# VectorE takes its branch over the general program six operations before its last one, and SyncE issues the last store

## The chip, the core and the metric

The kernel runs on one NeuronCore of a Trainium2 chip. The core has five engines with an instruction stream each: TensorE (PE in the profile, its weight loads PEld), VectorE (DVE), ScalarE (ACT), GpSimd (POOL) and SyncE (SP), which does nothing but issue DMAs and wait. The metric is the device time of one launch in microseconds; lower is better.

## The reference

The input is 2048 rows of 448 features in bf16. The kernel computes `h2 = h + B(LN(h))` with `h = x + A(LN(x))`, where

- A is sliding-window attention: 16 heads of 28, each row looks at 8 rows of its past, two apart, and the result goes through a 448 x 448 matrix;
- B is an MLP mixer: layer norm, a 448 x 448 matrix and gelu, a shift of each quarter of the features by -1, +1, -2 or +2 rows, a second 448 x 448 matrix, a residual; then layer norm, 448 x 1792, gelu, 1792 x 448, and a residual.

```python
h  = x + A(layernorm(x), A_wqkv, A_wo)
z  = layernorm(h)
x1 = z + shift(gelu(layernorm(z) @ w1)) @ w2
h2 = h + x1 + gelu(layernorm(x1) @ w3) @ w4
```

The change touches the order of instructions, and none of the arithmetic.

## The kernel before, in words

The program holds two versions of the computation. The **fast program** (`_fast_path`, L452) takes a short cut in the chain of layer norms that holds for ordinary numbers. It also computes a **flag** (`phase_flag`, L969): whether any variance was infinite or not a number. The **general program** (`_general_path`, L1072) makes no such assumption. Every engine runs its part of the fast program to the end, reads the flag from SBUF into a register (L1514), and jumps over its part of the general program when the flag is zero (L1515). With these inputs the flag is zero. So each engine makes one taken branch, across as many instructions as its part of the general program has. For SyncE these are the DMAs of the general program: 17 in each of four attention stages (L1318 to L1323), 16 stores, and the loads. VectorE, ScalarE and above all TensorE have more.

After the branch comes `finish` (L1484): an engine that issued output stores waits until they have landed. Then all five engines meet in a barrier at the end of the block (L1508): each drains and counts up a semaphore, GpSimd waits for all of them and releases them.

The fast program is written as operations with dependencies. A list scheduler (`_Sched.schedule`, L234) puts them in an order by its own cost estimates and by ranks written out by hand (L1042 to L1068). `_emit_plan` (L416) then finds the semaphore waits, and `emit` (L1468) writes each engine's instructions; all of them carry the line L1476 in the profile.

The end of the fast program is the second MLP matrix, `phase_W4` (L949). For each group of 128 rows, TensorE runs 14 matmuls (one for each 128 of the 1792 hidden features) into one PSUM bank of 128 x 448; VectorE adds the residual and writes bf16 to `xb` (L961); a DMA stores the rows. For the last 512 rows (`u == 3`) each group has a store of its own (L963). The very last group is cut in two halves of 224 columns. SyncE stores the first half, ScalarE's queue the second:

```python
dma("out%d_%d_%d" % (m, a, n0), bass.AP(out.tensor, ...), xb[:, i, n0:n1],
    128 * n * 2, q="sp" if n0 == 0 else "act")
```

TensorE's last nine groups feed VectorE's last nine operations, which are all residual adds. I call them add 1 to add 9; adds 8 and 9 are the two halves. The planner gives the groups two PSUM banks in turn, so that TensorE's group 6 waits until VectorE has done add 4, and so on. ScalarE's last activation ends about 20 us before the end, and GpSimd has finished about 57 us before it.

Of the kernel before, what the change touches and what calls it, by code (L numbers as in the profile page):

```python
# [415 lines left out]
def _emit_plan(S, order, sems, chan_sems):  # L416
    cnt = {}
    for e, lst in order.items():
        c = 0
        for op in lst:  # L420
            if op.is_dma:
                k = cnt.get(op.chan, 0) + 1
                cnt[op.chan] = k
                op.sem = chan_sems[op.chan]; op.val = 16 * k
            elif op.users > 0:
                c += 1
                op.sem = sems[e]; op.val = c
    eclock = {e: {} for e in order}
    plan = {}
    for op in S.gorder:  # L430
        cur = eclock[op.eng]
        waits = []
        for d in sorted(op.deps, key=lambda d: -d.t1):
            key = id(d.sem)
            if cur.get(key, 0) >= d.val:
                continue
            waits.append((d.sem, d.val))
            new = dict(cur)
            for k2, v2 in d.clock.items():
                if new.get(k2, 0) < v2:  # L440
                    new[k2] = v2
            cur = new
        eclock[op.eng] = cur
        plan[op.idx] = waits
        oc = dict(cur)
        if op.sem is not None:
            oc[id(op.sem)] = max(oc.get(id(op.sem), 0), op.val)
        op.clock = oc
    return plan


def _fast_path(nc, es, flag, A_x, A_wqkv, A_wo, B_w1, B_w2, B_w3, B_w4, out):  # L452
# [9 lines left out]
    S = _Sched()  # L462
# [51 lines left out]
    def dve(meth, dur, **kw):  # L514
        return S.add("dve", meth, dur, **kw)
# [17 lines left out]
    def dma(chan, out_ap, in_ap, nbytes, dur=450.0, rate=200.0, q="sp", after=(), bulk=False, lat=1200.0):  # L533
        if chan[0] == "w":
            chan = ch(chan)
        op = S.macro(q, [("dma_start", dict(out=out_ap, in_=in_ap))], dur, chan=chan, lat=(lat, nbytes / rate, 1150.0),
                     after=tuple(after) + tuple(last) if chan[0] in "xw" else after, bulk=bulk)
        if chan[0] in "xw":
            last[:] = [op]
        if chan[0] == "o":  # L540
            op.deps -= {d for d in op.deps if d.is_dma}
        return op

    def tile(n=1):
        g = _Group(n)
        return lambda fn: _PV(g, lambda b: fn(ps[:, b:b + n, :]))

    def mm(out_ap, lhsT, rhs, start, stop, **kw):
        return ("matmul", dict(out=out_ap, lhsT=lhsT, rhs=rhs, start=start, stop=stop, **kw))

    def pe(ins, dur, mode, after=()):
        return S.macro("pe", ins, dur, mode=mode, after=after)
# [3 lines left out]
    def xrows(ap, m):  # L556
        return bass.AP(ap.tensor, 256 * m * D, [[2 * D, 128], [1, 2 * D]])
# [391 lines left out]
    def phase_W4(u):  # L949
        for k in range(2):  # L950
            m = 2 * u + k
            for a in range(2):
                S.tag = "W4_%d_%d" % (u, k)
                i = 2 * m + a
                for n0, n1 in ((0, 224), (224, D)) if (u, k, a) == (3, 1, 1) else ((0, D),):
                    n = n1 - n0
                    T = tile()
                    ins = [mm(T(lambda p, n=n: p[:, 0, 0:n]), h3T[u % 2][:, f, a, 128 * k:128 * k + 128], w4_s[:, f, n0:n1], f == 0,
                              f == NF - 1) for f in range(NF)]
                    w4s.append(pe(ins, 14 * (n / 2.4 + 2.5), "full", after=w4s if n < D else ()))  # L960
                    dve("tensor_tensor", (150 + n) / 0.96, out=xb[:, i, n0:n1], in0=T(lambda p, n=n: p[:, 0, 0:n]),  # L961
                        in1=xb[:, i, n0:n1], op=ALU.add)
                    if u == 3:  # L963
                        dma("out%d_%d_%d" % (m, a, n0), bass.AP(out.tensor, 256 * m * D + a * D + n0, [[2 * D, 128], [1, n]]), xb[:, i, n0:n1],
                            128 * n * 2, q="sp" if n0 == 0 else "act")
            if u < 3:
                dma("out%d" % m, xrows(out, m), xb[:, 2 * m:2 * m + 2, :].rearrange("p a n -> p (a n)"), 128 * D * 4)

    def phase_flag():  # L969
        S.tag = "flag"  # L970
        bits = mv[:, 1, :, :].rearrange("p i s -> p (i s)").bitcast(I32)
        dve("tensor_scalar", 150, out=fint[:], in0=bits, scalar1=23, scalar2=255, op0=ALU.logical_shift_right,
            op1=ALU.bitwise_and)
        dve("tensor_reduce", 180, out=fmax[:], in_=fint[:], axis=AX.X, op=ALU.max)
        dve("tensor_scalar", 120, out=fbit[:], in0=fmax[:], scalar1=254.5, scalar2=None, op0=ALU.is_ge)
        T = tile()
        w4s.append(pe([mm(T(lambda p: p[0:1, 0, 0:1]), fbit[:], ones[:, 0:1], True, True)], 60, "c32"))
        return dve("tensor_scalar", 200, out=flag[0:1, 0:1], in0=T(lambda p: p[0:1, 0, 0:1]), scalar1=16.0,
                   scalar2=None, op0=ALU.mult)
# [45 lines left out]
    phase_W3(0)  # L1025
    wo_ln2(3, 4)
    phase_W4(0)
    wo_ln2(5, 6)
    phase_W1(3, 4)
# [3 lines left out]
    w2_ln3(4, 5)  # L1033
    phase_W1(7, 1)
    phase_W4(1)
    flag_op = phase_flag()
    w2_ln3(6, 7)
    phase_W3(2)
    phase_W4(2)
    phase_W3(3)  # L1040
    phase_W4(3)
# [419 lines left out]
def _plan(nc, es, S, prefix):  # L1461
    order = S.schedule()
    S.settle()
    sems = {e: es.enter_context(nc.semaphore(prefix + "sem_" + e)) for e in order}
    chan_sems = {c: es.enter_context(nc.semaphore(prefix + "d_" + c)) for c in S.chan_count}
    plan = _emit_plan(S, order, sems, chan_sems)

    def emit(e, eng):  # L1468
        out_final = {}
        for op in order.get(e, []):  # L1470
            if op.load is not None:
                eng.preload_act_table_set(_TABLE_SETS[op.load])
            for (sem, val) in plan[op.idx]:
                eng.wait_ge(sem, val)
            for meth, kw in op.ins:
                inst = getattr(eng, meth)(**kw)  # L1476
            if op.is_dma:
                inst.then_inc(op.sem, 16)
                if op.chan.startswith("out"):
                    out_final[op.chan] = max(out_final.get(op.chan, 0), op.val)  # L1480
            elif op.users > 0:
                inst.then_inc(op.sem, 1)

        def finish():  # L1484
            for c, v in out_final.items():
                eng.wait_ge(chan_sems[c], v)
        return finish
    return emit
# [5 lines left out]
def bass_sequential_preLN__sliding_local_dilated__mixer_s_mlp__prompt_kernel(  # L1494
    nc, A_x, A_wqkv, A_wo, B_x, B_w1, B_w2, B_w3, B_w4, out,
):
    args = (A_x, A_wqkv, A_wo, B_w1, B_w2, B_w3, B_w4, out)
    with ExitStack() as es:
        flag = es.enter_context(nc.sbuf_tensor("flag", [1, 1], I32))
        gate = es.enter_context(nc.semaphore("gate"))  # L1500
        with ExitStack() as es1:
            S, flag_op = _fast_path(nc, es1, flag, *args)
            flag_op.users += 1
            emit_fast = _plan(nc, es, S, "f_")
            _LAST["S"] = S
        with ExitStack() as es2:
            emit_general = _plan(nc, es, _general_path(nc, es2, *args), "g_")
            with nc.Block() as block:  # L1508
                for e in _ENG:
                    def body(eng, e=e):  # L1510
                        finish = emit_fast(e, eng)
                        eng.wait_ge(flag_op.sem, flag_op.val)
                        with eng.register("redo_" + e) as reg:
                            eng.reg_load(reg, flag[0:1, 0:1])  # L1514
                            with eng.If_ne(reg, 0):  # L1515
                                finish()
                                eng.drain().then_inc(gate, 1)
                                eng.wait_ge(gate, len(_ENG))
                                emit_general(e, eng)()
                        finish()  # L1520
                    getattr(block, _ENG[e])(body)

# [27 lines left out]
```

## Time and profile before

| | |
|---|---|
| runs | 199.91, 201.06, 201.94, 202.78 us; median 201.5 us |
| profiled execution, its own time | 201.94 us |
| profiled execution, span from the first to the last instruction | 200.2 us |
| around the span | 1.7 us |
| TensorE matmul busy | 186.1 us (93%) |
| VectorE busy | 119.8 us (60%) |
| ScalarE busy | 105.8 us (53%) |
| GpSimd busy | 49.9 us (25%) |
| instruction packets, queue q8 | 27, 0.44 MB |
| instruction packets, queue q14 | 8, 0.07 MB |

Busy time counts work on data alone. Register loads, branches, waits and the issuing of DMAs are an engine's sequencer's work; the profile lists them by source line with an engine name that ends in q (DVEq, ACTq). The difference of two starts on such lines tells how long the engine stood between them. Queues q1 and q10 carry SyncE's and ScalarE's data, q8 and q14 carry instructions that are fetched for the engines.

### The profile page before, as it was taken

Reading aid. Unit: us, or ns where it says so; the run is one execution under the profiler, and the core shown is the slowest. Engines: PE = TensorE matmul, PEld = TensorE weight load, DVE = VectorE, ACT = ScalarE, POOL = GpSimd, SP = SyncE. Lnnn points to the kernel's source line nnn. Section 1 sums busy time; section 2 is a strip of 40 time slices with the busy share of each in tenths; the row PEclk is TensorE's granted clock in tenths of the full one; section 3 lists DMA queues with packets and bytes.
Section 4 is the critical chain, followed back from the end, with each engine's and each line's share of the span. In section 5 each row is a group of like instructions: output and inputs, shape, how many; then the busy total and the mean of one; then the engine's idle time right before and its main releaser. Section 6 shows DMA issues by size and latency. Waiting matters only on the chain.

```text
span 200.2 us, 6997 instructions
## 1 busy us (share of the span) xinstructions
PE 186.1 (93%) x3150; PEld 117.6 (59%) x3151; DVE 119.8 (60%) x294; ACT 105.8 (53%) x120; POOL 49.9 (25%) x89
## 2 busy tenths in 40 slices
PE   7789999999997998979998999999999999999990
PEld 2458666455453464538854465588887558755570
DVE  6899797677999249999998039998000210021130
ACT  3586799975699688485631731156466006600000
POOL 6211430000082000594633002979500000000000
PEclk9999999999999699999999999999999999999999
DMA  6967575444368423355452300424400011001111
GB/s 182 362 238 104 114 157 100 141 120 127 99 129 131 128 66 114 108 101 135 137 96 46 95 0 0 93 49 101 89 0 3 0 46 49 3 0 46 69 46 37
DMA packets 31851, 18.32 MB, mean 92 GB/s; under 512 B 21640, under 2 KB 31240, under 8 KB 31816
## 3 DMA queue, kind: packets, MB, share of 16 engines
q1 hardware_dynamic: 31128, 17.30, 35.1%
q8 instruction: 27, 0.44, 1.0%
q10 hardware_dynamic: 688, 0.52, 0.9%
q14 instruction: 8, 0.07, 0.1%
HBM read 9.75 MB, written 1.84 MB: 58 GB/s over the span
## 4 chain that ended last, share of the span: by engine, by line
PE 53%; DVE 27%; DMA 8%; POOL 6%; issue 1%; ACT 1%; DVEq 0%
PE ps L1476 53%; DVE st L1476 8%; DMA HT<-ln 7%; DVE xb L1476 5%; DVE ln L1476 4%; POOL rstd L1476 4%; DVE xin L1476 2%; POOL xb L1476 2%; DVE QK L1476 2%; DVE mv L1476 2%; DVE nmr L1476 1%; DVE arena L1476 1%; DMA xin<-in_A_x_dram 1%; DVE pt L1476 1%; DVE w_s L1476 1%
## 5 line engine op out<-in xcount | busy, mean ns | idle before, releaser
L1476 PE MATMUL ps<-HT,w_s 64*128 64x256 bf16 (+3 forms) x952 | 57.7, 280 | 2.6 <-DMA HT<-ln 2.3
L1476 PEld LDWEIGHTS ps<-HT,w_s 64*128 64x128 bf16 x952 | 45.3, 95 | 14.7 <-DMA HT<-ln 3.3
L1476 DVE TENSOR_TENSOR xb<-ps,xb 128x448 bf16<-128x448 f32 (+2 forms) x25 | 18.6, 747 | 57.2 <-PE ps L1476 57.2
L1476 PE MATMUL ps<-HT,arena 64*128 64x128 bf16 (+2 forms) x448 | 27.2, 270 | 0.6 <-DMA HT<-ln 0.4
L1476 POOL TENSOR_SCALAR vtmp<-mv 128x2 f32<-128x2 f32 x30 | 6.1, 203 | 84.5 <-DVE mv L1476 78.8
L1476 ACT ACTIVATE arena<-ps 128x1024 bf16<-128x1024 f32 x14 | 14.3, 1024 | 16.9 <-PE ps L1476 16.9
L1476 PE MATMUL ps<-w_s,h 128*128 128x448 bf16 x112 | 21.9, 353 | 0.0
L1476 PE MATMUL ps<-w_s,arena 128*128 128x448 bf16 (+1 forms) x126 | 21.7, 332 | 0.0
L1476 POOL TENSOR_TENSOR rstd<-vtmp,mhalf 128x2 f32<-128x2 f32 x30 | 21.0, 701 | 2.3
L1476 ACT ACTIVATE QK<-ps 128x1024 bf16<-128x1024 f32 (+2 forms) x19 | 18.6, 979 | 5.6 <-PE ps L1476 5.3
L1476 PEld LDWEIGHTS ps<-HT,arena 64*128 64x128 bf16 x448 | 16.6, 94 | 8.3 <-DMA HT<-ln 0.9
L1476 ACT ACTIVATE h<-ps 128x1024 bf16<-128x1024 f32 x14 | 14.3, 1023 | 8.2 <-PE ps L1476 8.2
L1476 DVE BATCH_NORM_STATS2 st<-xin 128x6 f32<-128x448 bf16 x32 | 18.4, 609 | 0.4 <-DMA xin<-in_A_x_dram 0.4
L1476 PEld LDWEIGHTS ps<-w_s,arena 128*128 128x128 bf16 x126 | 12.2, 98 | 9.2 <-issue 0.2
L1476 PEld LDWEIGHTS ps<-w_s,h 128*128 128x128 bf16 x112 | 10.9, 98 | 10.3 <-issue 0.2
L1476 POOL TENSOR_TENSOR xb<-xb,xin 128x448 bf16<-128x448 bf16 x16 | 16.1, 1034 | 1.0 <-DVE ln L1476 1.0
L1476 ACT ACTIVATE pt<-ps 128x912 bf16<-128x912 f32 x18 | 15.7, 927 | 1.2 <-PE ps L1476 1.1
L1476 PE MATMUL ps<-wo_s,QK 128*128 128x448 bf16 x64 | 13.0, 353 | 1.7 <-DVE xin L1476 1.3
L1476 DVE TENSOR_TENSOR QK<-ps,lnz 128x456 bf16<-128x456 f32 (+1 forms) x24 | 10.8, 507 | 6.3 <-PE ps L1476 6.2
L1476 PE MATMUL ps<-wv_s,HT 64*128 64x448 bf16 x126 | 13.1, 350 | 0.6 <-DVE wv_s L1476 0.6
L1476 PE MATMUL ps<-w_s,QK 112*128 112x448 bf16 x64 | 12.6, 353 | 0.0
L1476 DVE TENSOR_SCALAR ln<-xin,mv,rstd 128x448 bf16<-128x448 bf16 x25 | 11.8, 496 | 0.6 <-ACT rstd L1476 0.6
(67 smaller groups left out, 190.6 us busy)
## 6 DMA issues: line engine op xcount, KB each, us to landing
w_s<-in_B_w_dram SPq DMA_DIRECT2D x19, 224.0 KB, 2.6
xin<-in_A_x_dram SPq DMA_DIRECT2D x7, 224.0 KB, 6.5
out_dram<-xb SPq DMA_DIRECT2D x6, 224.0 KB, 2.8
vu<-vt SPq DMA_DIRECT2D x9, 128.0 KB, 2.7
h<-in_A_wqkv_dram SPq DMA_DIRECT2D x3, 336.0 KB, 5.2
wv_s<-in_A_wqkv_dram SPq DMA_DIRECT2D x2, 336.0 KB, 6.6
w_s<-in_B_w_dram SPq DMA_DIRECT2D x2, 336.0 KB, 3.2
wo_s<-in_A_wo_dram SPq DMA_DIRECT2D x4, 98.0 KB
```

What stands on the lines that cost most here:

```text
L1476: inst = getattr(eng, meth)(**kw)
```

## The change

The store of the second half goes to SyncE's queue like all other stores. For VectorE alone, the fast program is cut in front of its last six operations. The register load and the branch come at the cut. The six operations stand twice in the program: at the head of the general branch, and behind it under the opposite condition. The other engines branch at their end as before.

```diff
                     if u == 3:
                         dma("out%d_%d_%d" % (m, a, n0), bass.AP(out.tensor, ...), xb[:, i, n0:n1],
-                            128 * n * 2, q="sp" if n0 == 0 else "act")
+                            128 * n * 2)
...
-    def emit(e, eng):
+    def emit(e, eng, lo=0, hi=None):
         out_final = {}
-        for op in order.get(e, []):
+        for op in order.get(e, [])[lo:hi]:
...
             emit_fast = _plan(nc, es, S, "f_")
+            dve = [op for op in S.gorder if op.eng == "dve"]
+            late = max(len(dve) - 6, dve.index(flag_op) + 1)
...
                     def body(eng, e=e):
-                        finish = emit_fast(e, eng)
+                        cut = late if e == "dve" else None
+                        finish = emit_fast(e, eng, 0, cut)
                         eng.wait_ge(flag_op.sem, flag_op.val)
                         with eng.register("redo_" + e) as reg:
                             eng.reg_load(reg, flag[0:1, 0:1])
                             with eng.If_ne(reg, 0):
+                                if cut is not None:
+                                    emit_fast(e, eng, cut)
                                 finish()
                                 eng.drain().then_inc(gate, 1)
                                 eng.wait_ge(gate, len(_ENG))
                                 emit_general(e, eng)()
+                            if cut is not None:
+                                with eng.If_eq(reg, 0):
+                                    emit_fast(e, eng, cut)
                         finish()
```

## The prediction

> **What bounds the kernel now.** I first read the chain of waits for the last 60 us. It is one piece of TensorE work that ends in VectorE's last add:
>
> ```profile
> 5 pieces in order of time: start us, us, what
> ...
> 141.82 53.72 PE ps L1476 x574
> 195.54 0.02 issue
> 195.56 0.39 DVE xb L1476
> ```
>
> From 141.8 to 195.5 TensorE runs without a hole, and the work on data ends at 195.95. The span ends at 200.2. So there are two places to look at: the 4.3 us behind the last add, where this change acts, and the rhythm of the last adds, into which it puts a branch. The timeline of the last stretch shows the rhythm:
>
> ```profile
> 182.29 0.62 DVE L1476 TENSOR_TENSOR xb<-ps,xb 128x448 bf16<-128x448 f32 x1 [2.02 <-PE ps L1476]
> ...
> 184.94 0.62 DVE L1476 TENSOR_TENSOR xb<-ps,xb 128x448 bf16<-128x448 f32 x1 [2.02 <-PE ps L1476]
> 187.58 0.63 DVE L1476 TENSOR_TENSOR xb<-ps,xb 128x448 bf16<-128x448 f32 x1 [2.02 <-PE ps L1476]
> ...
> 195.56 0.39 DVE L1476 TENSOR_TENSOR xb<-ps,xb 128x224 bf16<-128x224 f32 x1 [0.95 <-PE ps L1476]
> 195.99 0.36 ACTq L1476 DMA_DIRECT2D out_dram<-xb  x1
> ```
>
> These are adds 3, 4, 5 and 9 and the last store. VectorE works 0.62 us and waits 2.02 us for TensorE. Third, the instructions of the register load, the branch and the final barrier, by line:
>
> ```profile
> L1514 SPq TENSOR_LOAD <-flag x1: 525/525/525, 195.0 to 195.0; - x1
> L1514 DVEq TENSOR_LOAD <-flag x1: 546/546/546, 195.6 to 195.6; - x1
> L1514 ACTq TENSOR_LOAD <-flag x1: 474/474/474, 196.4 to 196.4; - x1
> ```
>
> ```profile
> L1515 PEldq COMPARE_BRANCH  x1: 4818/4818/4818, 194.3 to 194.3; - x1
> L1515 SPq COMPARE_BRANCH  x1: 63/63/63, 195.6 to 195.6; - x1
> L1515 DVEq COMPARE_BRANCH  x1: 72/72/72, 196.2 to 196.2; - x1
> L1515 ACTq COMPARE_BRANCH  x1: 59/59/59, 196.9 to 196.9; - x1
> ```
>
> ```profile
> L1508 SPq DRAIN  x1: 13/13/13, 199.0 to 199.0; - x1
> L1508 DVEq DRAIN  x1: 58/58/58, 199.1 to 199.1; - x1
> L1508 PEldq DRAIN  x1: 73/73/73, 199.2 to 199.2; - x1
> L1508 ACTq COMPARE_BRANCH  x1: 38/38/38, 199.8 to 199.8; - x1
> L1508 ACTq DRAIN  x1: 8/8/8, 200.0 to 200.0; - x1
> ```
>
> A branch counts as tens of ns, but the time to the engine's next instruction is the price: VectorE 196.16 to 199.08 and ScalarE 196.89 to 199.82, 2.92 us each; TensorE 4.82. SyncE branches at 195.60 and has its next instruction at 195.80, GpSimd's is 0.17 us behind its branch: 0.2 us or less. In the packet records a fetch of 8 KB on the instruction queue q14 starts 1.04 us behind VectorE's branch and 1.18 behind ScalarE's and takes 0.47 and 0.40 us, and the engine goes on 1.4 us after that. TensorE's has 16 KB on q8 and takes 2.03 us. So three engines jump to code that must be fetched, and two to code that is there.
>
> The engines reach the barrier in the order SyncE 199.00, VectorE 199.08, TensorE 199.21, ScalarE 199.98. **ScalarE is last.** Its chain is: add 9 ends 195.95, store issued 195.99 to 196.35, register load 196.39 to 196.86, branch 196.89, fetch to 199.82, drain 199.98, end of the span 200.22.
>
> **The change part by part.**
>
> *The store leaves ScalarE.* ScalarE's last activation ends at 175.26. Its load (0.47) and branch (2.92) then end before 179, 17 us before add 9, which covers them. Its entry at 199.98 vanishes. If the cover were gone it would pay the 3.4 us again.
>
> *The store joins SyncE.* SyncE's store of the first half was issued by 194.97, so its queue is free. It now waits for add 9, at 195.99, and issues in 0.33 us (its own row for the first half), to 196.32. Behind that wait stand its register load, its branch and its waits for the stores. Load 0.525: 196.88. Branch: 196.95, and 0.2 by its own row: 197.15. Then it waits for the landing. Before, 14 of the 16 parts of the last store had landed at 197.54 and the two last at 198.68 and 198.92, because those two DMA engines also carried TensorE's fetches. In SyncE's queue the store stands behind the first half, which landed at 198.76; before it was carried out behind that one too, from another queue. I leave the landing at 198.92; the bounds are 0.4 earlier (VectorE's fetch of 0.47 us is no longer beside it) and 0.3 later (56 KB, whose packets span about that time on the late engine). SyncE's drain began 0.24 behind its last landing, which gives 199.17.
>
> *VectorE's branch moves to the cut.* The cut is behind add 3. The register load was issued 0.01 us after add 9 had started, so now at 182.30; it ends at 182.85. Branch 182.88. The target is fetched: 2.92, to 185.81. The second branch is not taken: 0.2 by SyncE's row. Add 4 starts at 186.0 instead of 184.94 and ends at 186.6. Six adds are queued behind the branch. Who waits: SyncE's store of add 4 (1.1 us late; its next is due at 188.24, nothing collides), and TensorE, whose group 6 starts at 187.19 and needs the bank of add 4. That leaves 0.5 us of cover. Add 5 is due at 187.58 anyway. Cost: nothing. For the fetch the bounds are 2.9 us (VectorE's own row) and 4.8 (TensorE's); a gain here is excluded, since no add can start before its matmuls. I take 2.9: same engine, same jump.
>
> [...] If VectorE's fetch were like q8's, 4.8 us, it would go on at 187.7, add 4 would end at 188.5, and group 6 would start 1.4 us late. [...]
>
> *What VectorE gains at its end.* Its entry moves from 199.08 to about 196.1. TensorE enters at 199.21 either way, so this half of the change is worth nothing by itself.
>
> **Sum.** The last entry becomes TensorE's: its branch needs add 7 (end 193.50) and neither edit moves it. Its drain ends at 199.28, ScalarE's ended at 199.99: 0.71 us less. The profiled execution had 201.94 for a span of 200.2; with the same 1.7 us around it I get 201.94 - 0.71 = 201.23. It lies 0.44 above the median of the runs, so **on the scale of the median 201.5 becomes 200.8 us**.
>
> **The rivals.**
>
> *A, slower: the stall reaches TensorE.* [...] The place is the bank of add 4; it decides once VectorE resumes later than about 186.5, which is 3.7 us after its branch. Two fetches in series are 5.84: 188.7, add 4 ends at 189.55, and TensorE, with no hole until its end, is 2.4 us late. 200.8 + 2.4 = 203.2 us. For it: TensorE's row of 4.8 is beyond that point. Against it: VectorE's and ScalarE's rows agree at 2.92 with one packet each.
>
> *B, no change: SyncE inherits the fetch.* One DMA and one wait more stand in its stream; if its target falls out of what is loaded, it continues at 196.95 + 2.92 = 199.87, just where ScalarE did: 201.5 us. Against it: the jump grows by an instruction or two among some hundred.
>
> *C, more is gained.* With two fetches out of the last 4 us, the late store parts and TensorE's fetch of 2.03 us (undisturbed q8 packets took 0.9) may shorten, and part of the 1.7 us around the span may hold fetches of the closing code, whose packets stand at 199.7 to 201.2. The first is worth up to 0.5, the second at most about as much: 199.9 us. No view shows either.
>
> That the change doesn't do what it says is no real case: which engine branches where follows from the program.
>
> **How the numbers follow.** My forecast has a chance of 0.62, A 0.14, B 0.11, C 0.13. The four runs spread from 199.91 to 202.78, so a median carries about 0.7 us of its own. The range is 199.6 to 202.7: it takes in the forecast, B, most of C, and A at its lower bound of 1.4 us (202.2). One per cent, 2.0 us, is about what a measurement of this kernel can tell from no change. Faster than that needs C with luck: 0.07. Slower needs A at its full price or beyond: 0.11. Within it: 0.82.
>
> **What would show it.** Right: ScalarE's and VectorE's rows of the branch stand near 176 and 182.9; VectorE resumes 2.9 us later; add 4 starts near 186.0 and add 5 at its old place; TensorE's piece has no hole; the drains stand in the order ScalarE, VectorE, SyncE, TensorE, the last at 199.2, and the span is 199.5. Wrong: idle time of TensorE before group 6 (A); SyncE's first wait on L1486 only near 199.9 (B); TensorE's drain well before 199.0 (C). A hole anywhere before 182 would mean that something else moved.

## The result, and the profile after

The changed kernel takes 197.83 us (median of 12 runs, 196.49 to 202.29), the kernel before beside it 201.06 us (17 runs). The ratio is 0.989, 95% interval 0.985 to 0.993. Compared a second time, the ratio was 0.9935 (0.9907 to 0.9962). So the change saves 1.3 to 2.2 us, where I had forecast 0.7. On the scale of the 201.5 us shown above, the first comparison gives 199.3 us, below my range. The ratios count only executions within 1.5% of the fastest of their kernel; the profiled ones of before and of `pe_plus12` (below) are slower than that, so of these two only the end and the time outside the span are used.

The chain of waits for the last stretch, of the kernel after (start, length, what):

```profile
...
139.94 53.33 PE ps L1476 x570
...
193.29 0.39 DVE xb L1476
```

TensorE has no hole from 139.9 to 193.3, so VectorE's branch in the middle of the adds cost TensorE nothing. The timeline shows where the branch stands, with adds 3, 4, 5 and 9:

```profile
180.01 0.62 DVE L1476 TENSOR_TENSOR xb<-ps,xb 128x448 bf16<-128x448 f32 x1 [2.02 <-PE ps L1476]
...
183.52 0.62 DVE L1476 TENSOR_TENSOR xb<-ps,xb 128x448 bf16<-128x448 f32 x1 [2.88 <-PE ps L1476]
185.31 0.63 DVE L1476 TENSOR_TENSOR xb<-ps,xb 128x448 bf16<-128x448 f32 x1 [1.16 <-PE ps L1476]
...
193.29 0.39 DVE L1476 TENSOR_TENSOR xb<-ps,xb 128x224 bf16<-128x224 f32 x1 [0.95 <-PE ps L1476]
```

Add 4 starts 3.51 us behind add 3 instead of 2.65, so it is 0.86 late. Add 5 stands 5.30 behind add 3, which is twice 2.65: on time. Now the branches (L1518 here) and the entries into the last barrier (L1510):

```profile
L1518 ACTq COMPARE_BRANCH  x1: 50/50/50, 172.5 to 172.5; - x1
L1518 DVEq COMPARE_BRANCH  x1: 72/72/72, 180.6 to 180.6; - x1
L1518 PEldq COMPARE_BRANCH  x1: 3420/3420/3420, 191.9 to 191.9; - x1
L1518 SPq COMPARE_BRANCH  x1: 62/62/62, 195.0 to 195.0; - x1
```

```profile
L1510 ACTq DRAIN  x1: 81/81/81, 175.1 to 175.1; - x1
L1510 DVEq DRAIN  x1: 430/430/430, 193.3 to 193.3; - x1
L1510 PEldq DRAIN  x1: 72/72/72, 195.4 to 195.4; - x1
...
L1510 SPq DRAIN  x1: 13/13/13, 195.8 to 195.8; - x1
```

The order is the one I had named, except that SyncE comes last and TensorE, which I had put at the end, arrives 0.4 before it. And both are much closer to the end of the work. I count from the start of add 9 on, because the two profiles differ by 2.27 us before it, in stretches that the change doesn't touch. (The profiled execution of before had one stretch of 3.4 us at a granted TensorE clock of 0.5, that of after had none; but this isn't shown to be the reason, for `act_early`, further down, had such a stretch too and reached add 9 at 192.41.) From add 9 to the end of the span it is 4.66 us before (195.56 to 200.22) and 2.89 after (193.29 to 196.18). I call this the tail. It is 1.77 us shorter; my sum had 0.71. The difference is in the arrivals that stood under ScalarE's: TensorE's branch took 4.82 us before and 3.42 after, though its instructions are the same, and SyncE's drain begins 2.49 us behind add 9's start instead of 3.44.

### The profile page after: what moved, and what is told of

Same layout as the page of the kernel before. It is cut to its first block, busy times and chain, and to the rows that moved or that the text cites. A ratio compares the mean times of both kernels' runs of the same rounds, so it can differ in the third digit from the quotient of the medians.

```text
span 196.2 us, 6997 instructions
## 1 busy us (share of the span) xinstructions
PE 184.9 (94%) x3150; PEld 117.6 (60%) x3151; DVE 119.6 (61%) x294; ACT 105.6 (54%) x120; POOL 50.1 (26%) x89
## 3 DMA queue, kind: packets, MB, share of 16 engines
HBM read 9.75 MB, written 1.84 MB: 59 GB/s over the span
## 4 chain that ended last, share of the span: by engine, by line
PE 46%; DVE 33%; DMA 8%; POOL 8%; ACT 3%; issue 2%; DVEq 0%
PE ps L1476 46%; DVE st L1476 10%; DMA HT<-ln 6%; DVE ln L1476 5%; DVE xb L1476 5%; POOL rstd L1476 4%; DVE xin L1476 3%; DVE QK L1476 2%; POOL xb L1476 2%; DVE mv L1476 2%; DVE nmr L1476 2%; ACT pt L1476 2%; DMA xin<-in_A_x_dram 1%; DVE arena L1476 1%; POOL vtmp L1476 1%
## 5 line engine op out<-in xcount | busy, mean ns | idle before, releaser
L1476 PE MATMUL ps<-HT,w_s 64*128 64x256 bf16 (+3 forms) x952 | 56.0, 275 | 2.0 <-DMA HT<-ln 2.0
L1476 PEld LDWEIGHTS ps<-HT,w_s 64*128 64x128 bf16 x952 | 44.8, 94 | 13.0 <-DMA HT<-ln 2.7
```

## The experiments

All times below that begin with + are counted from the start of add 9 and are taken from the trace to a hundredth.

### Each half alone, and both kernels again

`store_only` has the first hunk of the diff and not the rest:

```diff
-                            128 * n * 2, q="sp" if n0 == 0 else "act")
+                            128 * n * 2)
```

> The store half alone; VectorE branches at its end as before. Measured from the start of add 9, the engines entered the last barrier before the change at +4.42 (ScalarE), +3.64 (TensorE), +3.52 (VectorE), +3.44 (SyncE), and after it SyncE was last at +2.49. Theory S (the barrier waits for the slowest of four independent arrivals, so each half alone leaves one 2.9 us code fetch at the end): VectorE or TensorE is last at +3.5 to +3.7, the tail from the start of add 9 to the end of the span is 3.75 to 3.9 us instead of 4.66, ratio 0.996. Rival H (the store half holds the whole gain, since only ScalarE was last): tail near 2.9 us, ratio 0.989.

`dve_only` has the rest and not the first hunk; the heart of it:

```diff
...
+                        cut = late if e == "dve" else None
+                        finish = emit_fast(e, eng, 0, cut)
...
+                            if cut is not None:
+                                with eng.If_eq(reg, 0):
+                                    emit_fast(e, eng, cut)
...
```

> The VectorE half alone; the last store stays on ScalarE's queue. Theory S: ScalarE stays last at +4.4, tail 4.6 to 4.7 us, ratio 1.000 within its interval; add 4 is about 1.1 us late and TensorE has no hole. Rival H': if taking VectorE's fetch away makes the other engines' fetches and the late store parts faster, ScalarE's arrival is earlier than +4.2 and the ratio is 0.997 or less.

`after_again` and `before_again` have no edit.

> The changed kernel, nothing different. Theory S: SyncE last again at +2.4 to +2.6, tail 2.9 us, ratio 0.989 to 0.992. Rival U (the gain in the first comparison was partly a difference of the runs before the tail): ratio 0.996 or more. On TensorE: its branch took 4.82 us in the profile of before, where a second packet of 16 KB stood just ahead of the fetch, and 3.42 in that of after, where it was missing. If the change is the reason, 3.4 again here; if it is chance, it can be 4.8 here.

> The kernel before, nothing different. Ratio 1.000, which also tells what the comparison can resolve. ScalarE last at +4.4, tail 4.6 to 4.7 us. On TensorE's branch: 4.8 us with two packets of 16 KB if the change is the reason for its shorter branch after; 3.4 us with one packet if that is chance.

| kernel | 16 KB packets at TensorE's branch | TensorE | SyncE | VectorE | ScalarE | tail | ratio (95% interval) |
|---|---|---|---|---|---|---|---|
| before, first profile | 2 | +3.64 | +3.44 | +3.52 | +4.42 | 4.66 | |
| before_again | 1 | +2.38 | +2.27 | +3.54 | +4.09 | 4.33 | 1.001 (0.998 to 1.005) |
| store_only | 2 | +3.44 | +3.51 | +3.47 | early | 3.91 | 0.9985 (0.995 to 1.002) |
| dve_only | 1 | +2.56 | +2.43 | +0.01 | +4.04 | 4.28 | 0.9997 (0.997 to 1.003) |
| after, first profile | 1 | +2.12 | +2.49 | +0.01 | early | 2.89 | 0.989 (0.985 to 0.993) |
| after_again | 2 | +3.47 | +3.52 | +0.01 | early | 3.92 | 0.9935 (0.991 to 0.996) |

The engine columns are the starts of the drains at the barrier. Two things follow.

First, **neither half moves the time measurably alone**. With the store half, TensorE, VectorE and SyncE stand together at the end, in the lines of the barrier of `store_only`:

```profile
L1508 PEldq DRAIN  x1: 73/73/73, 196.4 to 196.4; - x1
L1508 DVEq DRAIN  x1: 59/59/59, 196.5 to 196.5; - x1
L1508 SPq DRAIN  x1: 13/13/13, 196.5 to 196.5; - x1
```

With the VectorE half ScalarE is last as ever, in those of `dve_only`:

```profile
L1510 DVEq DRAIN  x1: 432/432/432, 194.3 to 194.3; - x1
...
L1510 ACTq DRAIN  x1: 8/8/8, 198.4 to 198.4; - x1
```

Rival H (the store holds the whole gain) fell in time: 0.989 lies well outside the interval of `store_only`, and 0.9935 outside by little, with its own interval overlapping. Its tail alone would not have told: with two packets it is 3.91 us, and 3.92 with both halves. That tail, 0.75 shorter than before's, and the time outside the span (further down) would make the store half worth up to 0.9 us; the time shows 0.3, with 0.9 at the edge of the interval. Rival H' fell as a gain in time: ScalarE is 0.05 earlier than in `before_again`, which has the same single packet.

Second, **TensorE's branch has two forms, in the same kernel**. The kernel before shows the short one in its second profile (lines of the branch and of the barrier):

```profile
L1515 PEldq COMPARE_BRANCH  x1: 3674/3674/3674, 192.4 to 192.4; - x1
```

```profile
L1508 SPq DRAIN  x1: 13/13/13, 196.0 to 196.0; - x1
L1508 PEldq DRAIN  x1: 73/73/73, 196.1 to 196.1; - x1
L1508 DVEq DRAIN  x1: 57/57/57, 197.3 to 197.3; - x1
...
L1508 ACTq DRAIN  x1: 8/8/8, 197.8 to 197.8; - x1
```

and the changed kernel the long one in its second:

```profile
L1518 PEldq COMPARE_BRANCH  x1: 4678/4678/4678, 192.1 to 192.1; - x1
```

```profile
L1510 PEldq DRAIN  x1: 73/73/73, 196.9 to 196.9; - x1
L1510 SPq DRAIN  x1: 13/13/13, 196.9 to 196.9; - x1
```

So the change isn't the reason for the short branch. What goes with it stands in the DMA view (the instruction queue q8 with packets, MB and share). The kernel before had two packets of 16 KB at its end in the first profile, 194 to 196 us:

```profile
q8 instruction: 2, 0.03, 11.9%
```

and one in the second, 191 to 195.5 us:

```profile
q8 instruction: 1, 0.02, 1.3%
```

For the changed kernel, the last three stores follow with KB each and median us from issue to landing. In the first profile, with the short branch, 191 to 195 us:

```profile
q8 instruction: 1, 0.02, 1.6%
...
out_dram<-xb SPq DMA_DIRECT2D x1, 224.0 KB, 1.9
out_dram<-xb SPq DMA_DIRECT2D x2, 56.0 KB, 2.3
```

In the second, with the long branch, 191 to 195.5 us:

```profile
q8 instruction: 2, 0.03, 5.3%
...
out_dram<-xb SPq DMA_DIRECT2D x1, 224.0 KB, 4.7
out_dram<-xb SPq DMA_DIRECT2D x2, 56.0 KB, 3.4
```

I take the later packet for the branch's own fetch: it starts 1.23 us behind the branch in the first profile of before, and the only one of the first profile after starts 1.04 behind. With two packets it takes 2.15 us here instead of 1.00, and parts of the stores are late too: the 224 KB store, which is issued before the branch, lands in 4.7 us instead of 1.9. SyncE waits for these stores, so it is late with TensorE. In this form the change saves 4.66 - 3.92 = 0.74 us of the tail; with one packet 4.33 - 2.89 = 1.44.

The records of single packets show data packets that were slow while instruction packets were under way. The 224 KB store goes out in 128 packets of 1,792 bytes, which took 0.08 us at the median in every profile. In the three profiles with two instruction packets, three of the 128 took 0.26 to 0.42 us, while those packets were under way; in the other ten none took more than 0.09. The records don't name the DMA engine of a packet; that a late part and a fetch shared one, as the prediction has it, is inferred from their times.

### Where the extra packet stands

The q8 packet ahead of these starts about 22 us before add 9 in these profiles. Up to it q8 has 24 packets in each, one for every 251 to 252 recorded instructions of TensorE on average. TensorE's last nine groups with the register load and the branch are 254 instructions. So the branch seems to stand close to where the next packet is due. The expectations call such a packet a page, and put the place at 256 instructions; this was an estimate from these numbers, and no run shows 256. Two kernels move the branch by 12 instructions. `pe_minus12` leaves out six warm-up matmuls that nothing reads; `pe_plus12` issues the first six twice (the same edit on the kernel before is `before_plus12`, and `pe_plus12_b` is `pe_plus12` again):

```diff
+        extra = [op.idx for op in order.get('pe', []) if op.tag == 'warm' and not op.users][-6:]
...
+            if op.tag == "warm" and op.idx in extra:
+                continue
```

```diff
+        extra = [op.idx for op in order.get('pe', []) if op.tag == 'warm'][:6]
...
-            for meth, kw in op.ins:
+            for meth, kw in op.ins * (2 if op.tag == "warm" and op.idx in extra else 1):
```

> The changed kernel, with six of TensorE's twenty warm-up matmuls left out where nothing reads them, so that its stream is 12 instructions shorter ahead of the branch. In six profiles TensorE's branch took 3.4 to 3.9 us three times, with one 16 KB fetch behind it, and 4.6 to 4.8 three times, when a second 16 KB packet had started 0.2 us behind the branch; the packet before that always stands 22.2 us ahead of add 9, which is some 256 instructions. Theory B (the branch stands right at a page boundary of 256 instructions, and whether the next page is asked for before the branch is chance): 12 instructions fewer keep the boundary out of reach; one packet, branch 3.4 to 3.9 us, SyncE last, tail 2.9 us, ratio 0.989 or less if the missing warm-up costs nothing. Rival M (it is memory contention or chance in the fetch, wherever the boundary lies): two packets as often as before, in about half the profiles.

> The changed kernel, with the first six warm-up matmuls issued twice: TensorE's stream is 12 instructions longer ahead of the branch, in a stretch in which TensorE waits for the first input anyway. Theory B: the boundary is now always crossed before the branch. Then either the next page is always asked for just ahead of the branch and its packet stands in the way of the branch's own fetch (two packets, branch 4.6 us or more, tail 3.9 us, ratio 0.995), or it is asked for so much earlier that it is nearly through. Rival M: one packet in about half the cases.

> The kernel before with the first six warm-up matmuls issued twice, as in pe_plus12: TensorE's page request then comes 2 us earlier and is through before the branch. Theory: one packet behind the branch, TensorE at +2.3 to +2.6, ScalarE still last at +4.0 to +4.2, tail 4.2 to 4.4 us against 4.66 with two packets; ratio 0.998 to 1.000. Against pe_plus12 (0.993) this gives the change's gain with TensorE in its short form: 4.3 - 2.8 = 1.5 us, 0.75%.

> The changed kernel with the longer warm-up again, on the chip of before_plus12. Theory: one packet behind the branch again, tail 2.7 to 3.0 us, ratio 0.991 to 0.993, and 0.006 to 0.008 under that of before_plus12. If the early packet was chance, two packets can stand at the branch again and the tail is 3.9.

| kernel | q8 packets start at | TensorE's branch | tail | ratio (95% interval) |
|---|---|---|---|---|
| after_again | -1.04, -0.20 | 4.68 | 3.92 | 0.9935 (0.991 to 0.996) |
| after, first profile | -0.32 | 3.42 | 2.89 | 0.989 (0.985 to 0.993) |
| pe_minus12 | -0.29 | 3.77 | 2.95 | 0.993 (0.990 to 0.996) |
| pe_plus12 | -3.10, -0.36 | 3.60 | 2.76 | 0.993 (0.990 to 0.996) |
| pe_plus12_b | -3.08, -0.38 | 3.96 | 3.13 | 0.993 (0.990 to 0.996) |
| before_plus12 | -3.15, +0.23 | 4.04 | 4.29 | 1.003 (1.000 to 1.005) |

Twelve instructions more move the extra packet 2 us ahead, in all three profiles, where it is through before the branch. So it moves with TensorE's stream. In the unchanged layout it starts 0.2 us behind the branch (194.52 and 194.33 in the first profile of before), and it appeared in 3 of the 8 profiles of that layout. Why it is sometimes there and sometimes not is open; so is the share of the timed runs that have it, which the times don't tell. With 12 instructions fewer it was absent, in one profile, which a share of a third would often give by chance.

In time the longer warm-up gains nothing against the changed kernel (0.993 beside 0.9935 and 0.989); it may cost a little itself (1.003 for `before_plus12`, interval 1.000 to 1.005). But it lets both kernels be compared with one packet each: 0.993 to 1.003 is 2.0 us, where the tails say 4.29 less 2.76 or 3.13, 1.2 to 1.5 us, and the time outside the span 0.3 more (1.84 less 1.57 or 1.56): 1.4 to 1.8 us, which agrees with 2.0 within the two intervals of 0.3% either way.

### TensorE without a fetch

`pe_no_general` leaves TensorE's part of the general program out of the program, so that its branch jumps over a few instructions:

```diff
-                                emit_general(e, eng)()
+                                if e != "pe":
+                                    emit_general(e, eng)()
```

> The changed kernel with TensorE's part of the general program left out (it is not executed with these inputs, so the outputs are the same; with a set flag this program could not finish). TensorE's branch then jumps over a few instructions and fetches nothing. Theory L (once ScalarE's and VectorE's fetches are gone, TensorE's fetch sets the end in two ways: by its own arrival, and because the last parts of the last two stores land behind its 16 KB packet): TensorE arrives with its last matmul, no part of a store is late (all within 0.2 us of the first), SyncE's drain is at about +2.2 and the tail 2.5 to 2.6 us against 2.9 and 3.9, ratio 0.987 to 0.989. Rival: late parts stay near +2.3, so they are the stores' own, and the tail stays at 2.8 or more.

The branch takes 0.35 us, in the line of the branch, and the line of SyncE's drain follows:

```profile
L1518 PEldq COMPARE_BRANCH  x1: 350/350/350, 192.8 to 192.8; - x1
```

```profile
L1510 SPq DRAIN  x1: 13/13/13, 196.8 to 196.8; - x1
```

TensorE's drain ends with its last matmul, and yet the tail is 3.05 us and the ratio 0.992 (0.989 to 0.995), no better than the changed kernel. SyncE is last at +2.65, because the last part of the last store lands at +2.41, and its other 15 parts by +1.93. The theory expected no late part. But a q8 packet of 16 KB starts at -0.26 here too: the branch was over in 0.35 us, and the packet came all the same. So TensorE's arrival is worth nothing in this form, and the test of the late parts didn't take the suspected cause away. That the packets make the parts late thus rests on the other profiles, and on the slow packets shown above: all 16 parts of the 224 KB store land by -0.10 where no packet starts at -1.04, and the last one at +2.3 to +2.8 in the three profiles where one does.

### ScalarE's queue with an early branch

`act_early` keeps the last store on ScalarE's queue, and lets ScalarE, too, branch ahead of its last operation:

```diff
...
+            n_act = sum(op.eng == "act" for op in S.gorder)
...
-                        cut = late if e == "dve" else None
+                        cut = {"dve": late, "act": n_act - 1}.get(e)
...
```

> The changed kernel, but the last store stays on ScalarE's queue, and ScalarE branches ahead of that store, 20 us before the end, as VectorE does ahead of its six adds. In the profile of after, SyncE was last: its issue of the last store took 0.63 us (0.84 in the other profile), because it stands 1.34 us behind the first half on one queue, and the last part landed 1.8 us after the issue; on ScalarE's queue the same store took 0.36 to issue and its first parts landed 1.4 us after it. Theory: the landing is 0.2 to 0.3 us earlier, ScalarE arrives at +2.3 instead of SyncE at +2.5, tail 2.6 to 2.7 us where TensorE has one packet (against 2.9), 3.7 to 3.9 where it has two. Rival: nothing gained, since the late parts land by TensorE's fetch and not by the queue.

The tail is 2.99 us with one packet: TensorE +2.69, ScalarE +2.68, SyncE +2.57; the ratio is 0.991 (0.988 to 0.993), not to be told from the changed kernel. The store's first parts do land in 1.4 us, but the late part sets its end, at +2.50. The rival held. SyncE's issue of 0.63 to 0.84 us, from which I had taken the gain, was 0.33 in five other profiles with the store on SyncE and 0.42 in one, so it was no price of the queue.

### What the idle time hides

`cut1` moves VectorE's branch from six operations ahead of the end to one:

```diff
-            late = max(len(dve) - 6, dve.index(flag_op) + 1)
+            late = max(len(dve) - 1, dve.index(flag_op) + 1)
```

> The changed kernel with VectorE's branch one operation ahead of its end instead of six, between adds 8 and 9. Add 8 starts 1.34 us before add 9. If the branch costs what the profile of after shows (2.89 us to the next instruction and 0.1 for the second branch), add 9 starts 0.01 + 0.55 + 0.03 + 2.9 + 0.1 = 3.6 us behind add 8, 2.25 us late, and with it the last store: the span is about 2.2 us longer than that of the changed kernel with the same TensorE fetch, ratio 1.000 to 1.004. This is what the idle time before add 4 hides. If the fetch were cheaper close to the end, or prefetched, it would be less.

Adds 8 and 9 in the timeline of VectorE:

```profile
192.17 0.39 DVE L1476 TENSOR_TENSOR xb<-ps,xb 128x224 bf16<-128x224 f32 x1 [0.71 <-PE ps L1476]
196.01 0.39 DVE L1476 TENSOR_TENSOR xb<-ps,xb 128x224 bf16<-128x224 f32 x1 [3.45 <-issue]
```

Add 9 starts 3.84 us behind add 8 instead of 1.34: 2.50 late (expected 2.25; the register load took 0.77 instead of 0.55). The ratio is 1.0065 (1.003 to 1.010), 1.3 to 1.7% above the changed kernel and slower than before. The same branch is free six operations ahead and costs the whole change and more at one.

## Why the prediction was wrong

- *ScalarE is last, and its entry vanishes when the store leaves*: right. It enters at 175.1, 18 us before add 9, and nothing pays for its branch.
- *VectorE's branch in the adds costs nothing*: right. It came back 2.82 us after the branch (I had 2.92), add 4 was 0.86 late (1.06), add 5 on time, and TensorE had no hole. The longer stall that I had weighed, 4.8 us by TensorE's row with its 16 KB on q8, didn't come to VectorE, nor did rival A's two fetches in series (5.84), which no run shows. The q14 packet that starts 1.0 us behind VectorE's branch in the profile of after has 8 KB and took 0.61 us, and VectorE came back after 2.8 to 3.3 us in every profile with this cut.
- *SyncE doesn't inherit a fetch*: right. Its branch is 0.2 us in all kernels.
- *The last entry becomes TensorE's at 199.21, "neither edit moves it"*, and the landing stays at 198.92: **this is the step that failed**. No edit moves it, but it isn't a constant of the kernel, and the sum took it for one. The profile of before happened to hold the form with two packets; my sum knew only the one at -0.01, which took 2.03 us, and not the one at -1.04. In that form the sum is right to a few hundredths: 0.74 of the tail, against 0.71. In the other form TensorE is at +2.1 to +2.7, the stores land by +2.1 to +2.6, and the floor under ScalarE's entry is about a microsecond lower: the gain in the tail is 1.44.
- *VectorE's half is worth nothing by itself*: right as put, and misleading. With two packets VectorE's late entry hides under the others (3.91 with the store half, 3.92 with both). With one packet VectorE would be last at +3.5 after the store half, which makes a tail of 3.75 to 3.9 (the span ends 0.24 to 0.40 behind the last entry) against 2.89: 0.9 to 1.0 us. This is an estimate from VectorE's entries, since `store_only` was profiled with two packets only. The times point the same way, 0.9985 for the half and 0.989 and 0.9935 for the whole, but don't tell its size.
- *1.7 us around the span stay*: nearly. Own time less span is 1.55 to 1.64 in the eight profiles with the last store on SyncE (mean 1.58) and 1.72 to 1.85 in the five with it on ScalarE (mean 1.78), so the change gains 0.2 there; why is open. Rival C had named this place and TensorE's fetch, but gave the wrong cause for the latter: it expected it to shorten because two other fetches go.

Together the change is worth 0.74 + 0.2 = 0.9 us with two packets and 1.44 + 0.2 = 1.6 with one, or 0.5 to 0.8%. The second comparison's interval holds this; the first, 0.7 to 1.5%, holds its upper part. The rest of the first difference, and of the two profiled spans, isn't explained by these runs.

## What to carry to other kernels

A barrier at the end waits for the slowest of several arrivals, so list all of them, and take away every one that is late before asking what a single one is worth; here neither half could be measured alone. A branch over the general program cost TensorE, VectorE and ScalarE 2.5 to 4.8 us here (SyncE and GpSimd 0.2), and nothing in an idle stretch whose consumers could wait that long. And before a row of one profile is used as the floor of a sum, it wants a second profile of the same kernel: the floor here was one of two forms.

## What the hardware showed that I had not expected

- Data packets were slow while TensorE's instruction packets were under way: single packets of a store took 0.26 to 0.42 us instead of 0.08. Of the 16 parts of a store, 14 or 15 landed in 1.4 to 2 us, and the one or two others up to 4.8 us after the issue.
- TensorE's branch took 3.3 to 4.0 us with one 16 KB packet (five profiles) and 4.6 to 4.8 with two (three), in the same layout of code.
- TensorE's branch to code a few instructions ahead (0.35 us) was still followed by a 16 KB packet, at -0.26.
- A taken branch that was followed by an instruction packet of 8 KB cost 2.8 to 3.3 us on VectorE and 2.5 to 2.9 on ScalarE; one that no packet followed cost 0.2 us (SyncE, GpSimd).
